# Order of the products in a_out: by pair of heads, or all of one kind first

## The chip, the cores and the metric

The kernel runs on one core of a Trainium2 chip. Five engines work side by side, each on its own list of instructions: TensorE (matrix products; PE in the profile, and PEld for its loads of stationary weights), VectorE (DVE), ScalarE (ACT), GpSimd (POOL) and SyncE (SP, which here issues most of the DMA transfers). They wait for each other by semaphores. SBUF is the working memory, and PSUM, eight banks of 128 x 512 float32, takes the products of TensorE. The metric is device time in microseconds of one execution; less is better.

## The reference

A gated linear recurrence over 768 steps, for 4 batches and 8 heads of size 48, and then two MLPs on its 3072 rows of 384.

```python
for t in range(S):                      # S = 768; state is 48 x 48 for each batch and head
    state = f[:, :, t, :, None] * state + einsum('bhd,bhe->bhde', k[:, :, t], v[:, :, t])
    y[:, :, t] = einsum('bhd,bhde->bhe', q[:, :, t], state)
# x = y as 3072 rows of 384
x = softplus(x @ w_in) @ w_out          # 384 -> 2048 -> 384
x = mish(x @ w_in2) @ w_out2            # the same sizes, mish(h) = h * tanh(softplus(h))
```

f is a sigmoid of f_logit. All is float32.

## The kernel before

**The recurrence in chunks.** A group g is one chunk of 128 steps of one batch; chunk c = g // 4, batch g % 4, 24 groups in all. The eight heads lie as NP = 4 pairs: head 0 of a pair on partitions 0 to 47, head 1 on partitions 64 to 111. Within a group the recurrence is products: `a_scores` (L322) multiplies the scaled k and q of each head, `a_mask` (L335, DVE) keeps the lower triangle of these scores, `a_turn` (L346) and `a_state` (L361) make the contribution to the state, and `a_out` (L384 to L399) makes the outputs y: for each head the product of v with the masked scores (L389: 128 rows of the array, 64 columns, 128 moving columns), and from the second chunk on, added to it in PSUM, the product of the state of the chunk before with q (L397: 48 rows, 48 columns, 128 moving columns). The two heads of a pair write different partitions of one PSUM bank (0 to 63 and 64 to 127), and the four pairs write different columns of that bank. `a_outed` (L424, ACT) copies the bank out when the last product of the group is done. There are 20 groups with c > 0.

**The MLPs in units.** A unit is one layer, one block of 512 tokens and one block of 128 hidden features: 2 x 6 x 16 = 192 units. `m_h` (L467, L481) makes the hidden values, DVE and ACT apply softplus or mish to them and split the result into a high and a low part (`e_hi`, `e_lo`: ghi L496, glo L501), and `m_o` (L601, L611) multiplies these by the output weights. Products of large blocks are made of three products of 12-bit parts; the first eight units and all of the recurrence are plain float32, where every product has two rows on PE and two on PEld. The weights come as float64 bit patterns and are split on DVE and ACT (`split_a`, `split_b`: L139 to L151; `conv_away` for layer 2).

**What sets the order.** The groups of chunk c + 1 are made while the units of token block c run, four groups in the first 12 of 16 units (`plan_attn`: one group in 3 units; its `a_out` stands in the second of these). So the 20 groups with c > 0 lie in units 0 to 79. For these units each engine's list is set by a scheduler from the order in which the code is written and from modelled times; from unit 80 on, and in the steps before the first unit, the order is as written. The four instances of `a_out` for chunk 0 stand in the steps before the first unit and take v alone.

Of the kernel before, what the change touches and what calls it, by code (L numbers as in the profile page):

```python
# [20 lines left out]
NP = H // 2  # L21
# [3 lines left out]
KD = DM // 128  # L25
# [1 line left out]
R = 112  # L27
CAP = 2.0 ** 60
SAFE = 2.0 ** 40
# units are (layer, block of 512 tokens, block of 128 hidden features)  # L30
NAT = 8  # units of the first block whose products are plain float32
SPLITX = 5  # units before NAT at which its input is split
READY = 4  # weight blocks prepared before the first unit
AHEAD = 2  # units between the preparation of a weight block and its use
EARLY = 2  # units between its load and its preparation
LENT = (14, 12, 10, 8) * 3 + (14, 12, 14, 12)  # weight slots that stage a block of layer 1
SPAN = 8  # unit from which layer 2's weights are prepared
LEAD = 2  # units between their load and their preparation
HALVE = 1  # units between the split of a plain float32 block and its use
EVAC = 60  # L40
LAG = 4
LATE = 80  # from this unit on each engine's order is written out
PLACE = (12, 12, 15)
PLACE1 = (3, 3, 12)
HAND = {mybir.EngineType.Activation, mybir.EngineType.DVE, mybir.EngineType.PE}
# what is loaded first, in order: f, q and k ("k"), v of a group, weight block ("w")
LOADS = """
f0 k0 f1 k1 f2 f3 k2 v0 k3 v1 w0 v2 v3 w1 w2 w3 f4 k4 v4 f5 f6
"""
# the steps before the first unit: a letter of one() and a group or weight block  # L50
HEAD = """
h14 e0 P0 s0 e1 q0 P1 i0 s1 e2 k0 S0 q1 i1 P2 e3 k1 S1 p3 s2 i2 m0 o0 O0 h3 b0 q2 k2 S2 s3
i3 R0 m1 o1 O1 q3 k3 S3 m2 y2 A0 B0 O2 b1 R1 m3 y3 O3 b2 R2 C0 A1 B1 b3 R3 C1 t0 t1 A2 B2 T0
# [5 lines left out]
def recurrence__then__softplus_mish_mlps_kernel(  # L59
# [49 lines left out]
    n1 = len(tiles[1])  # L109
    tile_of = {c * B + b0 + j: k for k, (c, b0, nb) in enumerate(tiles[1]) for j in range(nb)}  # L110

    # ---------------------------------------------------------------- weights
    whi, wlo, w32 = {}, {}, {}

    raws = {}
# [17 lines left out]
        raws[layer, f] = raw, win  # L133

    def split_a(layer, f):
        """float64 -> its first 12 significant bits and what float32 keeps of the rest"""
        raw, win = raws[layer, f]
        s, m, sg = raw[:, :, 1], win[:, :, 1], raw[:, :, 0].bitcast(F32)
        act.activation(out=sg, in_=s, func=AF.Sign)  # L139
        dve.tensor_scalar(out=m, in0=m, scalar1=0x1FFFF, scalar2=None, op0=ALU.bitwise_and)  # L140
        dve.tensor_scalar(out=s, in0=s, scalar1=0x7FFFFE00, scalar2=None, op0=ALU.bitwise_and)
        act.activation(out=s, in_=s, func=AF.Relu, scale=8.0, bias=rebias)
# [14 lines left out]
        split_b(layer, f, hi, lo)  # L157

    def whole_a(f):
        """float64 -> float32"""  # L160
        raw, win = raws[1, f]
        s, m, e = raw[:, :, 1], win[:, :, 1], raw[:, :, 0]
        dve.tensor_scalar(out=e, in0=s, scalar1=0x7FF00000, scalar2=None, op0=ALU.bitwise_and)
        dve.tensor_scalar(
            out=m, in0=m, scalar1=0xFFFFFFF, scalar2=0x10000000,
            op0=ALU.bitwise_and, op1=ALU.bitwise_or,
        )
# [38 lines left out]
        whi[layer, f], wlo[layer, f] = w[:, 0], w[:, 1]  # L206
        return w[:, 0], w[:, 1]

    # -------------------------------------------------------------- attention
    G = {}  # L210

    def a_load_f(g):
# [170 lines left out]
    def a_out(g, pl=None):  # L383
        t = G[g]  # L384
        c = g // B
        t["yps"] = ps = bank(pl or ps_a, [128, NP, C])
        for p in range(KD if c == 0 else 0, NP):
            for i in range(2):
                pe.matmul(  # L389
                    ps[64 * i:64 * i + 64, p], t["v"][:, (2 * p + i) * D:(2 * p + i) * D + 64],  # L390
                    t["a", i][:, p],
                    start=True, stop=(c == 0),
                )
            if c:
                for i in (1, 0):
                    o = 64 * i
                    pe.matmul(  # L397
                        ps[o:o + D, p], t["sp"][o:o + D, p], t["q"][o:o + D, p],
                        start=False, stop=True,  # L399
                    )  # L400

    def a_rest(g):
# [39 lines left out]

    states = [const.tile([R, NP, D], F32, name=f"state{b}") for b in range(B)]

    # ------------------------------------------------------------------- MLPs
    xh, xl = {}, {}

    def split_x(key, kk):
# [194 lines left out]

        return [lambda c=c: part(c) for c in range(KD)]

    # --------------------------------------------------------------- schedule
    units = [(layer, k, f) for layer in (1, 2) for k in range(len(tiles[layer])) for f in range(NF)]
    index = {u: i for i, u in enumerate(units)}
    hooks = {}
# [6 lines left out]
            fn()  # L656

    def plan_prep(g, i):
        """the factors of group g over the units i-1 .. i+2"""
        at(i - 1, "act", a_exp, g)  # L660
        at(i, "dve1", a_scan, g)
        at(i, "act", a_inv, g)
        if g + 2 < NC * B:
            at(i, "act", a_load_f, g + 2)
        at(i + 1, "dve1", a_q, g)
        at(i + 2, "dve1", a_k, g)
        at(i + 2, "dve1", a_decay, g)

    def plan_attn(g, i):
        """the products of group g over the units i .. i+2"""  # L670
        at(i, "pe1", a_scores, g)
        at(i, "dve2", a_mask, g, 0)
        at(i, "dve2", a_mask, g, 1)
        at(i + 1, "pe1", a_turn, g)
        at(i + 1, "act", a_turned, g)
        at(i + 1, "pe2", a_out, g)
        at(i + 2, "act0", a_outed, g)
        if g < (NC - 1) * B:
            at(i + 2, "pe1", a_state, g)
            at(i + 2, "dve2", a_stated, g)  # L680
        if g + 2 < NC * B:
            at(i + 2, "dve2", a_load, g + 2)

    for k in range(1, n1):
        c, b0, nb = tiles[1][k]
        base = (k - 1) * NF
        for j in range(nb):
            g, i = c * B + b0 + j, base + 3 * j
# [5 lines left out]
        i = base + 3 * nb  # L694
# [21 lines left out]
    first = [k for k in range(n1) if tiles[1][k][0] > 0][0] * NF  # L716
    last = (n1 - 1) * NF
    for f in range(NF):
        if f >= READY:
            i = f - AHEAD  # L720
            at(max(i - EARLY, -1), "act0", load_w, 1, f)
            at(i, "dve1", whole_w if f < NAT else conv1, f)
        i = first + SPAN + (last - first - SPAN) * f // NF
# [89 lines left out]
    ]  # L813

    def late(i):
        """a unit of the second MLPs, each engine's instructions in the order written"""
        u = units[i] if i < n_units else None
        if u:
            m_h(u)
        t = [U[units[i - j]] if LATE <= i - j < n_units else None for j in range(4)]  # L820
        drain(u, LAG)
        ends = [fn for key in ended for fn in m_end_parts(*key)]
        place = PLACE1 if ended and ended[0][0] == 1 else PLACE
        ended.clear()
        run(i, "act0")
        steps = [
            (t[lag], fn2 if t[lag]["u"][0] == 2 else fn1) if t[lag] else (None, None)
            for lag, fn1, fn2 in STEPS
        ]
        for j, (x, fn) in enumerate(steps):  # L830
            for y, at_step in zip(ends, place):
                if at_step == j:
                    y()
            if x and fn:
                fn(x)
        for y, at_step in zip(ends, place):
            if at_step == len(steps):
                y()
        for where in ("pe1", "dve1", "act", "dve2", "pe2"):
            run(i, where)  # L840
        if u:
            pend.append(u)
# [43 lines left out]
    assert not hooks, sorted(hooks)  # L886
    main.close()

    # ------------------------------------- decays too steep for the products
    redo = nc.values_load(  # L890
        slow[0:1, 0:1], min_val=0, max_val=1, skip_runtime_bounds_check_because="it is 0 or 1"
    )
# [181 lines left out]
```

## Time and profile before

| | |
|---|---|
| median of 3 runs | 963.16 us (962.62 to 964.15) |
| span of the profiled execution, first to last instruction | 960.3 us |
| granted clock of TensorE, mean | 0.999 |
| PE busy, share of the span | 98% |
| DVE busy | 82% |
| ACT busy | 77% |

The profiled execution shows its span alone; the median of the runs lies 2.9 us above it, which is what an execution has around its first and last instruction. A busy PE is not PE at its peak: a product's row lasts until it has left the array, and rows that follow each other overlap, so what a product costs is read from start to start.

### The profile page before, as it was taken

The page shows a single profiled execution, that of the slowest core. Times are in us where ns is not written, and L with a number is a line of the kernel's source. Part 1 is how long each engine was busy: PE and PEld are TensorE (multiplying, and loading weights), DVE is VectorE, ACT ScalarE, POOL GpSimd, SP SyncE. Part 2 cuts the span into 40 slices and gives each one's busy share as a digit, 9 for nine tenths or more (in the row PEclk, how much of TensorE's full clock was granted, in tenths as well). Part 3 has the DMA queues.
Part 4 walks back from the last instruction along what each step waited for, and adds up shares of the span by engine and source line. Part 5 has one row for each costly group of instructions (what it writes and reads, how often), then busy time and mean ns, then how long its engine had stood idle before and what let it go on. Part 6 is the DMA issues. An engine that isn't in the chain of part 4 may idle for free.

```text
span 960.3 us, 13706 instructions
## 1 busy us (share of the span) xinstructions
PE 937.5 (98%) x4970; PEld 721.4 (75%) x4970; DVE 786.1 (82%) x1252; ACT 739.0 (77%) x1326; POOL 29.5 (3%) x84
## 2 busy tenths in 40 slices
PE   4999999999999999999999999999999999999997
PEld 4545767777777777877788888888888888888885
DVE  5999998988888888987677678787787887878875
ACT  4778896888788777866677678887788877887875
POOL 1000000000000000000003220000000000000000
PEclk9999999999999999999999999999999999999999
DMA  9799713354654746463008670100100201000001
GB/s 316 256 327 318 262 46 123 116 191 173 223 178 159 272 148 221 140 230 121 9 38 291 197 241 23 67 34 0 66 34 1 99 1 66 34 1 1 33 0 38
DMA packets 35117, 122.33 MB, mean 127 GB/s; under 512 B 4352, under 2 KB 7424, under 8 KB 35040
## 3 DMA queue, kind: packets, MB, share of 16 engines
q1 hardware_dynamic: 28704, 99.34, 29.8%
q0 software_dynamic: 6336, 22.02, 7.1%
q8 instruction: 41, 0.67, 0.3%
q14 instruction: 36, 0.29, 0.1%
HBM read 93.62 MB, written 26.74 MB: 125 GB/s over the span
## 4 chain that ended last, share of the span: by engine, by line
PE 93%; DVE 4%; issue 1%; ACT 1%; POOL 0%; ACTq 0%; POOLq 0%; DVEq 0%
PE po L611 39%; PE ps L481 39%; PE ps L389 3%; PE ps L397 3%; PE ps L322 2%; PE ps L467 2%; PE po L601 2%; PE ps L361 1%; PE ps L346 1%; PE busy L765 1%; DVE gg L256 0%; DVE a L335 0%; DVE w L147 0%; DVE d L518 0%; PE ps L407 0%
## 5 line engine op out<-in xcount | busy, mean ns | idle before, releaser
L481 PE MATMUL ps<-x,w 128*128 128x512 f32 x864 | 213.6, 392 | 0.0
L611 PE MATMUL po<-ghi,w 128*128 128x512 f32 x768 | 205.4, 398 | 0.0
L481 PEld LDWEIGHTS ps<-x,w 128*128 128x128 f32 x864 | 162.3, 188 | 36.3
L481 PE MATMUL ps<-xh,w 128*128 128x512 f32 x528 | 181.7, 399 | 2.1 <-DVE w L151 1.8
L611 PEld LDWEIGHTS po<-ghi,w 128*128 128x128 f32 x768 | 140.8, 188 | 31.1
L611 PE MATMUL po<-g,w 128*128 128x512 f32 x504 | 126.4, 395 | 0.0
L481 PEld LDWEIGHTS ps<-xh,w 128*128 128x128 f32 x528 | 98.8, 188 | 28.1 <-issue 3.4
L545 ACT ACTIVATE l<-d 128x512 f32<-128x512 f32 x96 | 60.7, 632 | 73.3 <-DVE d L541 73.3
L611 PE MATMUL po<-glo,w 128*128 128x512 f32 x384 | 112.4, 392 | 0.0
L611 PEld LDWEIGHTS po<-g,w 128*128 128x128 f32 x504 | 94.9, 188 | 21.9
L510 ACT ACTIVATE e<-ps 128x512 f32<-128x512 f32 x96 | 57.2, 596 | 70.1 <-PE ps L481 56.2
L481 PE MATMUL ps<-xl,w 128*128 128x512 f32 x264 | 103.1, 391 | 0.0
L501 DVE TENSOR_TENSOR glo<-l,ghi 128x512 fp32r<-128x512 f32 x128 | 87.8, 686 | 17.6 <-ACT ghi L496 16.7
L541 DVE TENSOR_SCALAR d<-ps 128x512 f32<-128x512 f32 x96 | 66.3, 691 | 37.3 <-PE ps L481 37.2
L555 DVE SCALAR_TENSOR_TENSOR l<-d,l 128x512 f32<-128x512 f32 x96 | 66.5, 692 | 33.1 <-ACT l L548 33.0
L496 ACT CAST ghi<-l 128x512 fp32r<-128x512 f32 x128 | 78.1, 610 | 14.4 <-DVE l L531 14.0
L518 DVE SCALAR_TENSOR_TENSOR d<-d,e 128x512 f32<-128x512 f32 x96 | 65.9, 687 | 26.5 <-ACT d L512 26.3
L611 PEld LDWEIGHTS po<-glo,w 128*128 128x128 f32 x384 | 72.1, 188 | 15.9
L578 DVE TENSOR_TENSOR l<-ps,l 128x512 f32<-128x512 f32 x96 | 66.4, 692 | 9.6 <-ACT l L575 0.9
L524 DVE TENSOR_TENSOR d<-l,d 128x512 f32<-128x512 f32 x96 | 65.9, 686 | 2.7
L570 DVE SCALAR_TENSOR_TENSOR l<-d,l 128x512 f32<-128x512 f32 x96 | 65.4, 682 | 0.0
L511 ACT ACTIVATE e<-e 128x512 f32<-128x512 f32 x96 | 60.7, 632 | 1.6
(107 smaller groups left out, 1306.0 us busy)
## 6 DMA issues: line engine op xcount, KB each, us to landing
raw<-in_w_dram SPq DMA_DIRECT2D x32, 768.0 KB, 6.2
w2d<-wo SPq DMA_DIRECT2D x32, 384.0 KB, 3.0
w<-w2d POOLq DMA_DIRECT2D x32, 384.0 KB, 3.9
raw<-in_w_dram SPq DMA_DIRECT2D x16, 767.9 KB, 10.3
win<-in_w_dram SPq DMA_DIRECT2D x16, 767.9 KB, 7.3
qk<-in_qkT_dram SPq DMA_DIRECT2D x22, 448.0 KB, 4.3
x2d<-o SPq DMA_DIRECT2D x12, 768.0 KB, 5.1
x<-x2d POOLq DMA_DIRECT2D x12, 768.0 KB, 5.8
```

What stands on the lines that cost most here:

```text
L481: pe.matmul(ps, w, r, start=(i == 0), stop=(i == len(steps) - 1))
L496: act.copy(out=t["hi"], in_=t["g"])
L501: dve.tensor_tensor(out=t["lo"], in0=t["g"], in1=t["hi"].bitcast(F32), op=ALU.subtract)
L511: act.activation(out=e, in_=e, func=AF.Exp, scale=-1.0)
L518: dve.scalar_tensor_tensor(out=d, in0=d, scalar=1.0, in1=t["e"], op0=ALU.subtract, op1=ALU.subtract)
L524: dve.tensor_tensor(out=d, in0=l, in1=d, op=ALU.subtract)
L541: dve.tensor_scalar(out=t["t"], in0=t["h"], scalar1=20.0, scalar2=None, op0=ALU.min)
L545: act.activation(out=t["l"], in_=t["t"], func=AF.Exp)
L555: dve.scalar_tensor_tensor(out=t["l"], in0=t["t"], scalar=-43.0, in1=t["l"], op0=ALU.max, op1=ALU.add)
L570: dve.scalar_tensor_tensor(out=t["l"], in0=t["t"], scalar=-1.0, in1=t["l"], op0=ALU.mult, op1=ALU.max)
L578: dve.tensor_tensor(out=t["l"], in0=t["h"], in1=t["l"], op=ALU.mult)
L611: pe.matmul(acc[c], w[layer, f][:, cols[c]], t[part], start=(f == 0 and part == "hi" and w is whi), stop=(f == NF - 1 and part == "lo"),)
```

## The change

In a group with c > 0 the eight products of v with the masked scores are issued first, over all four pairs, and then the eight products of the state with q. Before, each pair had its two products of v and then its two of the state. The flags follow: `start` (which makes a product overwrite instead of add) stands on the first pair alone, since it holds for the whole bank, and `stop` on the last. For chunk 0 nothing changes. The diff also takes comments out, which changes no instruction; lines below `a_out` move down by two.

```diff
         t["yps"] = ps = bank(pl or ps_a, [128, NP, C])
-        for p in range(KD if c == 0 else 0, NP):
+        first = 0 if c else KD
+        for p in range(first, NP):
             for i in range(2):
                 pe.matmul(
                     ps[64 * i:64 * i + 64, p], t["v"][:, (2 * p + i) * D:(2 * p + i) * D + 64],
                     t["a", i][:, p],
-                    start=True, stop=(c == 0),
+                    start=(p == first), stop=(c == 0),
                 )
-            if c:
+        if c:
+            for p in range(NP):
                 for i in (1, 0):
                     o = 64 * i
                     pe.matmul(
                         ps[o:o + D, p], t["sp"][o:o + D, p], t["q"][o:o + D, p],
-                        start=False, stop=True,
+                        start=False, stop=(p == NP - 1),
                     )
```

On TensorE, the first group with a state, which stands behind the products of unit 0. Before:

```order
L601 MATMUL po<-g,w_346 128x512
L389 MATMUL ps<-a,vt 64x128 x2
L397 MATMUL ps<-qk,sp 48x128 x2
L389 MATMUL ps<-a,vt 64x128 x2
L397 MATMUL ps<-qk,sp 48x128 x2
L389 MATMUL ps<-a,vt 64x128 x2
L397 MATMUL ps<-qk,sp 48x128 x2
L389 MATMUL ps<-a,vt 64x128 x2
L397 MATMUL ps<-qk,sp 48x128 x2
L361 MATMUL ps<-vt,kn 64x48
```

The same place now:

```order
L603 MATMUL po<-g,w_346 128x512
L390 MATMUL ps<-a,vt 64x128 x8
L399 MATMUL ps<-qk,sp 48x128 x8
L361 MATMUL ps<-vt,kn 64x48
L361 MATMUL ps<-vt,kn 48x48
```

Eight pieces became two; the products are the same, and so are the neighbours on both sides. The same holds for all 20 groups, and nothing else moves on TensorE.

On VectorE the order is the same but for one place, about unit 70, at the last block of layer 2's weights that is split (raw and win are its two copies, wo its parts). Before:

```order
L531 SCALAR_TENSOR_TENSOR l_4293<-ps_4277,d_4294 128x512
L335 TENSOR_TENSOR a_4368<-ps_4343,mask_100 128x512
L501 TENSOR_TENSOR glo_4322<-l_4293,ghi_4320 128x512
L518 SCALAR_TENSOR_TENSOR d_4358<-d_4358,e_4356 128x512
L335 TENSOR_TENSOR a_4370<-ps_4344,mask_100 128x512
L524 TENSOR_TENSOR d_4358<-l_4357,d_4358 128x512
L140 TENSOR_SCALAR win_4554<-win_4554 128x768
L531 SCALAR_TENSOR_TENSOR l_4357<-ps_4333,d_4358 128x512
L141 TENSOR_SCALAR raw_4553<-raw_4553 128x768
```

Now:

```order
L533 SCALAR_TENSOR_TENSOR l_4293<-ps_4277,d_4294 128x512
L141 TENSOR_SCALAR raw_4553<-raw_4553 128x768
L335 TENSOR_TENSOR a_4368<-ps_4343,mask_100 128x512
L503 TENSOR_TENSOR glo_4322<-l_4293,ghi_4320 128x512
L335 TENSOR_TENSOR a_4370<-ps_4344,mask_100 128x512
L140 TENSOR_SCALAR win_4554<-win_4554 128x768
L520 SCALAR_TENSOR_TENSOR d_4358<-d_4358,e_4356 128x512
L147 TENSOR_TENSOR wo_4670<-raw_4553 128x768
```

The steps of that split moved up, the first of them ahead of the first mask of a group; ScalarE's two steps of it (L139, L142) moved up likewise, and on SP's queue one load of v moved ahead of a store of weights.

## Rows read from the trace of the kernel before

**Rows 1.** The page: busy time, and the chain that ended last by engine.

```profile
PE 937.5 (98%) x4970; PEld 721.4 (75%) x4970; DVE 786.1 (82%) x1252; ACT 739.0 (77%) x1326; POOL 29.5 (3%) x84
PE 93%; DVE 4%; issue 1%; ACT 1%; POOL 0%; ACTq 0%; POOLq 0%; DVEq 0%
```

**Rows 2.** Stretches: from:to, length, busy PE, PEld, DVE, ACT, POOL (instructions), clock, DMA.

```profile
48.00:140.00 92.00, 88.97 (x509) 55.07 (x508) 89.20 (x150) 77.36 (x131) 0.45 (x4) 1.00 0.71 249
140.00:230.00 90.00, 90.00 (x563) 67.49 (x562) 81.80 (x135) 71.17 (x131) 0.45 (x4) 1.00 0.42 141
230.00:318.00 88.00, 88.00 (x560) 66.00 (x559) 76.84 (x128) 68.15 (x124) 0.45 (x4) 1.00 0.56 193
318.00:407.00 89.00, 89.00 (x564) 66.84 (x563) 78.45 (x133) 68.58 (x122) 0.83 (x5) 1.00 0.55 191
407.00:475.00 68.00, 68.00 (x412) 50.63 (x411) 50.52 (x80) 44.79 (x82) 0.22 (x2) 1.00 0.36 127
```

**Rows 3.** PE's waits for layer 1's weights, 48 to 475 us: us in total, times, longest.

```profile
PE ps L481 <- DVE w L151: 1.8, 1, 1.8
PE ps L481 <- DVE w L147: 0.3, 1, 0.3
```

**Rows 4.** Timeline of PE, one group's outputs: start us, us, engine, line, operation, shapes, count.

```profile
53.86 0.44 PE L389 MATMUL ps<-a,vt 128*64 128x128 f32 x4
54.23 0.42 PE L397 MATMUL ps<-qk,sp 48*48 48x128 f32 x4
54.58 0.44 PE L389 MATMUL ps<-a,vt 128*64 128x128 f32 x4
...
56.75 0.67 PE L361 MATMUL ps<-vt,kn 128*64 128x48 f32 x16
```

**Rows 5.** PE's instructions by line and shape: count, busy us, mean ns.

```profile
L397 PE MATMUL ps<-qk,sp 48*48 48x128 f32 x320 | 33.8, 288 | 0.0
```

**Rows 6.** Timeline of PE: longer runs of products of one shape, each with the next row.

```profile
31.02 0.86 PE L411 MATMUL ps<-a,qkv 128*48 128x128 f32 x12
31.81 0.98 PE L346 MATMUL ps<-ident,qk 112*128 112x112 f32 x8
...
77.37 1.16 PE L322 MATMUL ps<-qk 48*128 48x128 f32 x16
78.46 2.84 PE L601 MATMUL po<-g,w 128*128 128x512 f32 x6
```

**Rows 7.** Timeline of DVE: its idle time (in brackets) behind late softplus inputs, 48 to 96.

```profile
73.49 0.69 DVE L518 SCALAR_TENSOR_TENSOR d<-d,e 128x512 f32<-128x512 f32 x1 [0.99 <-ACT d L512]
...
80.11 0.69 DVE L518 SCALAR_TENSOR_TENSOR d<-d,e 128x512 f32<-128x512 f32 x1 [0.26 <-ACT d L512]
...
94.00 0.69 DVE L518 SCALAR_TENSOR_TENSOR d<-d,e 128x512 f32<-128x512 f32 x1 [0.21 <-ACT d L512]
```

**Rows 8.** Timeline: a low part as DVE makes it, and PE's first use of it.

```profile
308.90 0.69 DVE L501 TENSOR_TENSOR glo<-l,ghi 128x512 fp32r<-128x512 f32 x1
...
310.72 0.85 PE L611 MATMUL po<-glo,w 128*128 128x512 f32 x3
```

**Rows 9.** Timeline at the moved split: the load of raw, ScalarE's sign, a mask, its use.

```profile
431.11 0.38 SPq L128 DMA_DIRECT2D raw<-in_w_dram  x1
439.36 0.89 ACT L139 ACTIVATE raw<-raw 128x768 f32<-128x768 int32 x1
437.67 0.69 DVE L335 TENSOR_TENSOR a<-ps,mask 128x512 f32<-128x512 f32 x1
444.38 0.44 PE L389 MATMUL ps<-a,vt 128*64 128x128 f32 x4
```

**Rows 10.** DMA issues of 425 to 450 us: count, KB each, median us to landing.

```profile
raw<-in_w_dram SPq DMA_DIRECT2D x1, 768.0 KB, 6.0
```

**Rows 11.** Weight loads of the products of v: count, busy us, mean ns, idle before.

```profile
L389 PEld LDWEIGHTS ps<-a,vt 128*64 128x64 f32 x328 | 16.4, 134 | 19.6 <-issue 14.7 <-DVE raw L141 1.1 <-DVE raw L163 0.8
```

**Rows 12.** A cut of PE's timeline that ends at 55.75 us, inside a state piece.

```profile
55.67 0.31 PE L397 MATMUL ps<-qk,sp 48*48 48x128 f32 x2
```

## The prediction

> **What bounds the kernel now.** I read the page's first lines, then stretches of one token block each, then PE's timeline at one group's outputs, and at last what stands between PE and DVE. The page shows PE busy for 98% of the span and 93% of the chain that ended last on PE [rows 1]. The reader should not stop there, since the change works only from 53.9 to 464 us, and that part has two limits. From 140 to 475 us PE has no idle time at all, while DVE is busy for 81.80 of 90, 76.84 of 88, 78.45 of 89 and 50.52 of 68 us: PE alone sets the pace [rows 2]. From 48 to 140 us it is otherwise: DVE is busy for 89.20 of 92 us, 97%, and PE's only waits of some size, 0.3 and 1.8 us near 128 and 130 us, are for the high and low part of a weight block that DVE splits (L147, L151) [rows 2, 3]. That is a DVE with no room, and a PE that runs a little ahead and is caught at the end of the stretch.
>
> **What the order costs now.** A plain float32 product is two records on PE, and the two heads of a pair run beside each other: a cut in the middle of a state piece shows two records of 0.29 us each within 0.31 us [rows 5, 12]. So a piece of four records is two steps, one behind the other. A v piece takes 54.23 - 53.86 = 0.37 us and a state piece 54.58 - 54.23 = 0.35 us from start to start; the four pairs take 56.75 - 53.86 = 2.89 us [rows 4], that is 4 x 0.72. The same trace has a run of products that stay in one shape: the 12 records of L411 (v and scores again, 48 columns, two heads side by side) are six steps in 31.81 - 31.02 = 0.79 us [rows 6]. Against a state piece, which has the same 48 columns and two steps in 0.35, four steps more cost 0.44 us: 0.11 us for a further step. Two steps at 0.11 would be 0.22; so in every piece some 0.13 to 0.15 us belongs to the change of shape, eight times a group.
>
> **The change, part by part.** The v products become one run of eight steps, 0.37 + 6 x 0.11 = 1.03 us; the state products another, 0.35 + 6 x 0.11 = 1.01 us. Together 2.04 instead of 2.88, or 0.84 us less. There are 320 records of L397 at 16 a group, so 20 groups [rows 5]: 16.8 us less on PE. For the other end I take the longest run of another tiling, the 16 records of the scores, two halves of the rows beside each other: 78.46 - 77.37 = 1.09 us [rows 6]. With both runs at 1.09 the gain is 0.70 a group, 14.0 in all. I take 0.84, since L411 uses the array just as the v products do.
>
> The flags that change sit on the same instructions; I cost them at nothing, and no row lets me price them. The result leaves PSUM behind the last state product, as before, so ACT's copy of y moves with the end of the group.
>
> The moved split on DVE may wait: raw is issued at 431.11 and needs 6.0 us, so it lands near 437.1, and ScalarE's sign of it takes 0.89 us; the first mask behind it started at 437.67 [rows 9, 10]. The wait is about 438.0 + 0.5 for what runs ahead on ScalarE, less 437.6: under 1 us, and the products that read this mask start at 444.38, over 6 us later [rows 9]. Hidden. Without that cover it would be 1 us, once. The load of v that now stands ahead of a weight store on SP holds back a store that only layer 2 reads.
>
> One rule of the Trainium skill speaks against the gain. [rows 6] show that six steps with 128 rows of the array each go on at 0.11 us, weight loads included. The page "TensorE: Matmul & The Clock Gate", Part 3, The mechanism, says that a weight load overlaps matmuls in flight only where their row groups differ, which those of v never do. By that rule each further step would also pay its weight load; the price and time are the slower rival below. The trace does not agree.
>
> **What of it reaches the end.** In the first stretch four groups give PE 3.4 us. PE is then held by DVE, so the end of the stretch comes earlier only by the idle time of DVE that came from a late PE. Three such gaps are plain: ScalarE's 1 + e arrives late, because the hidden values came late, at 73.49, 80.11 and 94.00 us: 0.99 + 0.26 + 0.21 = 1.46 us [rows 7]. Two groups stand ahead of the first two (1.7 us less by then), three ahead of the third, so all three can close. I take 1.5 of 3.4; the ends are 0 and 2.8, all of DVE's idle time there (92 - 89.20 [rows 2]). So 1.9 us turn into a longer wait for L147 and L151 near 128 us.
>
> In the next three blocks PE would need 90, 88 and 89 less 3.4: 86.6, 84.6 and 85.6 us, still above DVE's busy time, by 4.8 us at least [rows 2]. What is late next is the low part glo. It is tightest in the last four units of a block, where no attention slows PE: the closest that I found ends at 308.90 + 0.69 = 309.59, and PE reads it at 310.72, 1.1 us later [rows 8]. DVE has 8.2, 11.2 and 10.6 us idle in these blocks [rows 2], much of it because it waits for products, and can make up most of the 3.4. If half is not made up, 1.7 - 1.1 = 0.6 us of wait comes in that block; I take 0.6 in all. At worst nothing is made up: 3.4 - 1.1 = 2.3 in each of three blocks, 6.9. In the fifth block DVE is at 50.52 of 68, and all passes.
>
> Sum: 16.8 - 1.9 - 0.6 = 14.3 us. The profiled execution's span of 960.3 becomes 946.0; with the 2.9 us that the median of the runs lies above the span, 948.9.
>
> **The rivals.**
> - All of it passes, because DVE's order has more air than its busy share says: 963.2 - 16.8 = 946.4. For it: PE is 98% busy and its waits for weights are 2.1 us in all. Against it: 97% DVE up to 140 us, with the weight split as the last releaser.
> - DVE becomes the bound in the next three blocks too: 16.8 - 1.9 - 6.9 = 8.0 us, 955.2. For it: 91% DVE in the second block, loads and ScalarE that it also waits for. Against it: no wait of PE there now, in over 250 us.
> - Slower: the weights are loaded between the steps, not beside them. Place: the two runs of each group; price: 0.13 us a step (134 ns [rows 11]) on 0.11, so 0.24. A group then takes 0.72 + 12 x 0.24 = 3.60, 0.72 more than now: 963.2 + 14.4 = 977.6. It decides from 0.18 us a step, where 0.72 + 12 x 0.18 = 2.88. Against it: L411 at 0.11.
> - The two heads' state products stop running side by side in the long run, as they share a bank: steps of 0.22, a state run of 0.35 + 6 x 0.22 = 1.67, with 1.03 2.70 a group, gain 0.18 x 20 = 3.6 us: 959.6. Against it: they already run side by side, in that bank [rows 12]. The Trainium skill's page "TensorEngine Tiling (Array Packing)", Gotcha 1: PSUM Pressure, says that different row tiles must not use one bank at the same time, which stands in its way; in this trace they do, on different partitions.
> - The gap between pieces is not the change of shape but what each piece needs anyway, and the run keeps 0.18 us a step: 963.2. Against it: L411 again.
>
> **How the numbers follow.** A run of this kernel tells a change from none at about 0.2%, 1.9 us. Chances: the forecast 0.60 (its own range 946.8, with 2.8 instead of 1.5 in the first stretch and no wait later, to 952), all passes 0.15, DVE bound 0.17, state products one by one 0.03, no gain 0.02, slower 0.03. Faster: 0.60 + 0.15 + 0.17 + 0.03 = 0.95; same 0.02; slower 0.03. The range takes in the first three, from 945.5 to 955.5: below by the error of 0.01 us in each reading (20 groups), above by the case of DVE. The last cases are left out.
>
> **What the profile after would show.** At the outputs of a group: two rows of 16 records, the v run about 1.03 us to the start of the state run, that one 1.01 to the next product. A step at 0.16 or more would speak for the weight loads. Near 128 us PE's wait for L147 and L151 should have grown from 2.1 to about 4 us, and DVE's three gaps should be gone; if PE's wait is as before, the first rival is right. From 140 to 410 us PE should wait for glo or for masks by under 1 us a block, and the blocks should be 3.4 us shorter; waits of 2 us a block mean the second rival. The forecast is wrong from the start if the two runs together take over 2.2 us, or if DVE's order hides a wait that I did not see.

## The result, and the profile after

| | before | changed |
|---|---|---|
| median of 4 runs each | 963.28 us (962.62 to 964.15) | 948.63 us (948.16 to 949.19) |
| ratio | | 0.984, 95% interval 0.983 to 0.986 |
| span of the profiled execution | 960.3 us | 947.2 us |
| that execution's own time | not on record | 948.94 us |

14.65 us went, 1.5%. The forecast was 948.9. In every run here whose time and span are both on record, the time lies 1.65 to 1.82 us above the span. The 2.9 us that "Time and profile before" gives for this compare the span of one execution with the median of others: the profiled execution of the kernel before was some 1.2 us shorter than the median.

The two runs of products came out as the working had them. The timeline of PE at the first group's outputs in the changed kernel (start us, us, engine, line, operation, shapes, count):

```profile
55.47 1.09 PE L390 MATMUL ps<-a,vt 128*64 128x128 f32 x16
56.50 1.08 PE L399 MATMUL ps<-qk,sp 48*48 48x128 f32 x16
57.51 0.67 PE L361 MATMUL ps<-vt,kn 128*64 128x48 f32 x16
```

Read from start to start: 1.03 us for v, 1.01 for the state, 2.04 together, where [rows 4] had 2.89. Over 20 groups that is 17.0 us of PE's time.

The page of the changed kernel, its lines of busy time and of the chain that ended last:

```profile
PE 922.5 (97%) x4970; PEld 727.1 (77%) x4970; DVE 784.7 (83%) x1252; ACT 738.2 (78%) x1326; POOL 29.5 (3%) x84
PE 88%; DVE 7%; issue 2%; ACT 2%; POOL 0%; POOLq 0%; ACTq 0%; DVEq 0%
```

Beside [rows 1], PE is busy for 15.0 us less with as many instructions. DVE has 7% of the chain instead of 4%. The stretches, cut at about the same places of the work as [rows 2]:

```profile
48.00:137.00 89.00, 85.57 (x498) 55.08 (x497) 88.59 (x149) 75.09 (x127) 0.45 (x4) 0.98 0.78 267
137.00:224.00 87.00, 87.00 (x564) 68.78 (x564) 80.73 (x133) 72.18 (x133) 0.45 (x4) 1.00 0.42 140
224.00:309.00 85.00, 85.00 (x561) 67.13 (x560) 76.28 (x127) 68.25 (x125) 0.45 (x4) 1.00 0.56 193
309.00:394.00 85.00, 85.00 (x562) 67.37 (x561) 77.66 (x131) 66.71 (x120) 0.83 (x5) 1.00 0.62 213
394.00:460.00 66.00, 66.00 (x419) 52.69 (x418) 52.37 (x85) 47.24 (x87) 0.40 (x2) 1.00 0.37 131
```

In the first, DVE is busy for 88.59 of 89 us, 99.5%, and PE's granted clock has a mean of 0.98. In the others PE is still never idle, although the blocks are 3.4 to 3.6 us shorter (table below). All that PE waits for between 48 and 475 us in the changed kernel (us in total, times, longest):

```profile
PE ps L483 <- DVE w L151: 2.3, 2, 1.8
PE po L603 <- DVE g L533: 0.9, 1, 0.9
PE ps L483 <- DVE w L147: 0.2, 1, 0.2
```

The second lies at 53 us, ahead of the first group; the kernel before has it too, at 51.5 us. The two others stand for [rows 3]: 2.5 us instead of 2.1. What DVE waits for in this stretch, first in the kernel before and then in the changed one:

```profile
DVE d L518 <- ACT d L512: 1.5, 3, 1.0
DVE glo L501 <- ACT ghi L496: 0.8, 2, 0.5
DVE raw L176 <- ACT raw L171: 0.3, 1, 0.3
```

```profile
DVE glo L503 <- ACT ghi L498: 0.2, 1, 0.2
```

The three gaps of [rows 7], 1.5 us, are gone, and most of the rest too. What is new stands behind the waits. The timeline of PE in the changed kernel, 122 to 137 us (in brackets idle time and what ended it):

```profile
122.72 0.73 PE L483 MATMUL ps<-xh,w 128*128 128x512 f32 x2 [0.55 <-DVE w L151]
...
126.85 0.50 PE L483 MATMUL ps<-xh,w 128*128 128x512 f32 x1 [0.19 <-DVE w L147]
...
129.39 0.73 PE L483 MATMUL ps<-xh,w 128*128 128x512 f32 x2 [1.80 <-DVE w L151]
...
131.30 2.77 PE L613 MATMUL po<-ghi,w 128*128 128x512 f32 x6
...
136.82 1.54 PE L613 MATMUL po<-ghi,w 128*128 128x512 f32 x6
```

The last two rows are the same six products of the same shapes, 2.77 us and 1.54 us. They had nothing to wait for; TensorE ran the first ones at half its clock. In the kernel before the same place of the work had the same wait and the full clock behind it:

```profile
130.52 0.73 PE L481 MATMUL ps<-xh,w 128*128 128x512 f32 x2 [1.80 <-DVE w L151]
...
132.24 1.54 PE L611 MATMUL po<-ghi,w 128*128 128x512 f32 x6
```

The granted clock from 131 to 135 us of the changed execution (columns as in the stretches):

```profile
131.00:135.00 4.00, 4.00 (x13) 3.12 (x12) 4.00 (x7) 3.93 (x9) 0.00 (x0) 0.59 0.00 0
```

The mean of 0.59 over 4 us is mostly 1.2 GHz instead of 2.4.

**Where the gain arises.** The table gives the start of some units in the two profiled executions (first row of the unit's hidden products on PE), and how much earlier the changed kernel is, counted from the start of unit 2. The count starts there because the changed execution came to unit 2 1.6 us later, ahead of the first group with a state. The same kernel run again (e11) came to it at 40.42 us, so this start varies from execution to execution. The spans hold it: they differ by 13.1 us.

| unit | before, us | changed, us | earlier by, us |
|---|---|---|---|
| 2 | 39.72 | 41.33 | 0 |
| 12 | 113.76 | 111.97 | 3.40 |
| 15 | 127.98 | 126.85 | 2.75 |
| 16 | 134.30 | 134.75 | 1.16 |
| 32 | 222.89 | 219.75 | 4.76 |
| 48 | 311.41 | 304.87 | 8.16 |
| 64 | 399.93 | 389.83 | 11.72 |
| 80 | 485.18 | 471.60 | 15.20 |

The first four groups bring all of 4 x 0.85 by unit 12. Of this 0.65 is gone at unit 15: 0.25 at unit 13, where the products with the high part start a little late behind ScalarE, and 0.40 in the waits for split weights of units 14 and 15 (0.55 and 0.19 us now, 0.33 before). From unit 15 to 16, where the wait is 1.80 us in both and the clock is down in one, 1.59 go. Then the four blocks bring 3.60, 3.40, 3.56 and 3.48. The end is 14.7 us earlier.

### The profile page after: what moved, and what is told of

It is laid out like the page before. It is cut to its first block, busy times and chain, and to the rows that moved or that the text cites. A ratio compares the mean times of both kernels' runs of the same rounds, so it can differ in the third digit from the quotient of the medians.

```text
span 947.2 us, 13705 instructions
## 1 busy us (share of the span) xinstructions
PE 922.5 (97%) x4970; PEld 727.1 (77%) x4970; DVE 784.7 (83%) x1252; ACT 738.2 (78%) x1326; POOL 29.5 (3%) x84
## 4 chain that ended last, share of the span: by engine, by line
PE 88%; DVE 7%; issue 2%; ACT 2%; POOL 0%; POOLq 0%; ACTq 0%; DVEq 0%
PE po L613 40%; PE ps L483 39%; PE ps L322 2%; PE ps L390 2%; PE ps L399 2%; PE ps L361 1%; PE ps L346 1%; PE ps L469 1%; DVE d L526 1%; PE busy L767 1%; DVE gg L256 1%; DVE a L335 1%; DVE w L147 1%; DVE d L520 1%; DVE raw L176 0%
## 5 line engine op out<-in xcount | busy, mean ns | idle before, releaser
L503 DVE TENSOR_TENSOR glo<-l,ghi 128x512 fp32r<-128x512 f32 x128 | 87.7, 685 | 14.2 <-ACT ghi L498 13.6
L514 ACT ACTIVATE d<-e 128x512 f32<-128x512 f32 x96 | 60.7, 632 | 1.7
```

Of the source, the lines that this page charges most:

```text
L503: dve.tensor_tensor(out=t["lo"], in0=t["g"], in1=t["hi"].bitcast(F32), op=ALU.subtract)
L514: act.activation(out=d, in_=e, func=AF.Identity, bias=1.0)
```

## The experiments

All gains below are read in the same way from the profiled execution of each kernel: us earlier than before at the start of a unit, counted from unit 2. Medians are of timed runs, and each stands beside the kernel before in runs of the same chip (963.28 us for the first row, 963.7 to 964.1 for the others); across chips, compare the ratios. In e4 to e8 the scheduler also put some of PE's products of units 13 to 20 in another order, so the columns 15 to 20 of these rows tell of that order too.

| kernel | 12 | 15 | 16 | 20 | 32 | 48 | 64 | 80 | end | median, us |
|---|---|---|---|---|---|---|---|---|---|---|
| changed | 3.40 | 2.75 | 1.16 | 2.11 | 4.76 | 8.16 | 11.72 | 15.20 | 14.69 | 948.63 |
| e1, two by two | 2.31 | 1.94 | 0.46 | 1.15 | 2.92 | 5.28 | 7.61 | 9.93 | 9.40 | 953.31 |
| e2, staggered | 1.15 | 1.08 | 1.09 | 1.36 | 2.27 | 3.47 | 4.67 | 5.81 | 5.84 | 959.11 |
| e3, filler | 3.38 | 2.56 | 2.25 | 3.20 | 5.85 | 7.98 | 9.72 | 13.20 | 12.71 | 949.63 |
| e4, changed, less DVE | 3.39 | 3.44 | 6.33 | 5.66 | 7.71 | 10.44 | 10.73 | 14.21 | 13.73 | 950.86 |
| e5, before, less DVE | 0 | 0.65 | 3.54 | 1.98 | 2.00 | 2.00 | 2.00 | 2.00 | 1.73 | 961.49 |
| e6, before, more DVE | 0 | -1.36 | -2.99 | 0.45 | -2.91 | -3.86 | -3.85 | -3.85 | -4.31 | 968.79 |
| e7, early split | 3.35 | 2.48 | 5.97 | 6.94 | 4.91 | 6.13 | 7.46 | 10.93 | 10.26 | 952.21 |
| e8, loads on POOL | 2.70 | 1.75 | 1.30 | 0.77 | -8.38 | -15.99 | -22.53 | -19.05 | -19.30 | 986.17 |
| e9, lead of 3 | 3.38 | 2.72 | 2.72 | 3.59 | 5.52 | 5.16 | 5.38 | 8.85 | 8.49 | 956.97 |
| e9, lead of 4 | 3.39 | 2.74 | 1.14 | 2.10 | 3.94 | 5.19 | 7.46 | 10.96 | 10.40 | 953.55 |
| e10, lead of 3 and filler | 3.38 | 2.57 | 2.69 | 3.61 | 4.70 | 5.85 | 2.29 | 5.77 | 5.41 | 956.02 |
| e11, changed again | 3.41 | 2.72 | 1.15 | 2.11 | 4.76 | 8.29 | 11.46 | 14.96 | 14.82 | 949.46 |

### What a piece costs: two by two, and staggered

The changed kernel's products, in two other orders. `with_v(p)` and `with_state(p, last)` issue the two products of one pair. In both, VectorE, ScalarE and SP keep the order of the kernel before: the split at unit 70 does not move.

```diff
+            steps = "v0 v1 s0 s1 v2 v3 s2 s3".split()      # e1_two_by_two
+            steps = "v0 v1 s0 v2 s1 v3 s2 s3".split()      # e2_staggered
+            for z, step in enumerate(steps):
+                if step[0] == "v":
+                    with_v(int(step[1]))
+                else:
+                    with_state(int(step[1]), z == len(steps) - 1)
```

> Order v0 v1, s0 s1, v2 v3, s2 s3 (v and s are a pair's two products with v and with the state): four pieces a group instead of eight before and two in the changed kernel. Theory, a fixed price of 0.143 us for each change of shape: a group takes 4 x 0.143 = 0.57 us less than before, 20 groups 11.4, so 951.9, or 953.5 if TensorE's clock falls near 131 us as in the changed kernel; a piece of four steps takes 0.37 + 0.22 = 0.59 (v) and 0.57 (state). Rival, the gap is a state product's wait for the v product just before it in the same columns: no such neighbours are left, so the full gain of the changed kernel, 948.6.

> Order v0 v1, s0, v2, s1, v3, s2 s3: six pieces a group, and no state product stands right behind the v product of its own columns. Theory, a price for each change of shape: two changes fewer than before, 2 x 0.143 x 20 = 5.7 us, so 957.6. Rival, the wait for the same columns: as the changed kernel, 948.6.

Two by two took 953.31 us (952.73 to 955.51), ratio 0.990 (0.988 to 0.992); staggered 959.11 us (956.85 to 960.22), ratio 0.995 (0.994 to 0.997). PE's timeline at the first group, two by two:

```profile
54.59 0.66 PE L391 MATMUL ps<-a,vt 128*64 128x128 f32 x8
55.18 0.64 PE L400 MATMUL ps<-qk,sp 48*48 48x128 f32 x8
55.75 0.66 PE L391 MATMUL ps<-a,vt 128*64 128x128 f32 x8
...
56.91 0.67 PE L361 MATMUL ps<-vt,kn 128*64 128x48 f32 x16
```

And staggered:

```profile
54.44 0.66 PE L391 MATMUL ps<-a,vt 128*64 128x128 f32 x8
55.03 0.42 PE L400 MATMUL ps<-qk,sp 48*48 48x128 f32 x4
55.38 0.44 PE L391 MATMUL ps<-a,vt 128*64 128x128 f32 x4
...
57.04 0.67 PE L361 MATMUL ps<-vt,kn 128*64 128x48 f32 x16
```

A group takes 56.91 - 54.59 = 2.32 us in four pieces and 57.04 - 54.44 = 2.60 in six. With 2.89 in eight and 2.04 in two, each piece that goes is worth 0.14 us, whichever columns stand behind each other. In neither order does a state product stand right behind the v product of its own columns, and the group still pays for each piece. So the price is not the sum in PSUM on columns just written. Nor is it the change of operands and bank alone: the MLPs' products of 12-bit parts change both without changing shape, and go on at 0.23 us from start to start. In the changed kernel:

```profile
113.80 0.39 PE L483 MATMUL ps<-xh,w 128*128 128x512 f32 x1
114.03 1.54 PE L613 MATMUL po<-ghi,w 128*128 128x512 f32 x6
115.41 0.85 PE L613 MATMUL po<-glo,w 128*128 128x512 f32 x3
```

(1.38 us for six, 0.23 for the one ahead of them.) That leaves the change between the two shapes of `a_out`; other pairs of shapes were not tried. At unit 80 staggered has 5.81 us, 20 x 0.29.

The times: two by two came to the 953.5 that was named for a clock that falls, and from unit 15 to 16 it loses 1.48 us. Staggered came out 1.5 us above its 957.6. Its two runs with a mean clock of 0.998 took 956.85 and 957.37 us, its three with 0.996 took 959.1 to 960.2. Both are far from the rival's 948.6.

### The clock: zero products in the gaps

Two products of 128 columns ahead of unit 14's hidden products and eight ahead of unit 15's, with a block of zeros (`none`), added to the bank without changing it. They run while PE would be idle. The scheduler moved four of the sixteen records of one group's scores (L322) into the same places; otherwise every engine keeps the order of the changed kernel.

```diff
+FILL = {(1, 0, 14): 2, (1, 0, 15): 8}
...
+            if i == 1:
+                for z in range(FILL.get(u, 0)):
+                    pe.matmul(ps[:, 0:128], ident, none, start=False, stop=False)
```

> The changed kernel with products of a zero block, which add nothing, in two hidden-value products of the first block: two at unit 14 and eight at unit 15 (0.22 us each, 0.43 and 1.7 us), in the place where TensorE waits for the low part of a weight block (0.55 and 1.80 us). Nothing becomes ready earlier. Theory, these idle stretches made the clock fall to half from 130.9 to 134.3 us: the clock stays at 1.00 and the time falls by 1.6 us to 947.0. Rival, the clock has nothing to do with it or falls for another reason (the longer runs of small products): the clock still falls and the time stays at 948.6, or rises by what the filler exceeds the waits.

The median is 949.63 us (949.05 to 950.69), ratio 0.985 (0.984 to 0.987). The first stretch of that kernel (columns as before):

```profile
48.00:137.00 89.00, 87.78 (x523) 57.73 (x522) 88.61 (x149) 76.24 (x129) 0.45 (x4) 1.00 0.74 264
```

The clock stays at 1.00, and the kernel is 1.09 us ahead of the changed one at units 16 and 32. From unit 15 to 16 it loses 0.31 us where the changed one loses 1.59; 0.19 more it had lost by unit 15. So in these executions the filler costs 0.5 us and saves 1.6. The clock came out as the theory had it, and the time, 949.63 instead of 947.0, did not. The lead goes: 7.98 against 8.16 at unit 48, 9.72 against 11.72 at unit 64. PE's waits in this kernel and the rows that lead to one of them:

```profile
PE po L618 <- ACT ghi L503: 2.4, 3, 1.5
```

```profile
376.23 0.89 ACT L141 ACTIVATE raw<-raw 128x768 f32<-128x768 int32 x1 [2.25 <-DMA raw<-in_w_dram]
377.15 0.56 DVE L143 TENSOR_SCALAR raw<-raw 128x768 int32<-128x768 int32 x1 [2.17 <-ACT raw L141]
...
385.30 1.65 PE L618 MATMUL po<-ghi,w 128*128 128x512 f32 x6 [1.52 <-ACT ghi L503]
```

A load of layer 2's weights lands, ScalarE has stood for it for 2.25 us and DVE for 2.17, and the high part of the hidden values behind them on ScalarE comes late. In the changed kernel the same load ended shorter waits:

```profile
374.05 0.89 ACT L139 ACTIVATE raw<-raw 128x768 f32<-128x768 int32 x1 [0.86 <-DMA raw<-in_w_dram]
374.96 0.56 DVE L141 TENSOR_SCALAR raw<-raw 128x768 int32<-128x768 int32 x1 [0.77 <-ACT raw L139]
```

ScalarE waits for these loads for 6.1 us between 225 and 400 us in the changed kernel and 8.9 with the filler. The clock's cost could be bought back, and bought nothing at the end. That it was the filler that kept the clock up rests on more than this one execution, since the clock also held once without it (below): the four runs with the filler have mean clocks of 0.997 to 0.999, the changed kernel's eight 0.995 to 0.998. It is no guarantee: with the filler and a lead of 3 two of five runs are at 0.995 and 0.996.

### DVE's share: less of it in both orders, more of it in the old one

Eight weight blocks of layer 1 are split with one step of DVE less: the mask of L140 is left out for them, and the bits that it clears stay in. This once with the changed order (e4) and once with the old one (e5). And the other way, the old order with that mask three times for blocks 14 and 15 (e6).

```diff
-        dve.tensor_scalar(out=m, in0=m, scalar1=0x1FFFF, scalar2=None, op0=ALU.bitwise_and)
+        if layer == 2 or not deep:                                          # e4, e5
+        for z in range(3 if layer == 1 and deep and f in (14, 15) else 1):  # e6
+            dve.tensor_scalar(out=m, in0=m, scalar1=0x1FFFF, scalar2=None, op0=ALU.bitwise_and)
```

> The changed kernel without one step of VectorE (the mask of the low bits, L140) in the split of layer 1's eight weight blocks: about 8 x 0.5 = 4 us less on VectorE before 130 us; the low parts of these weights are then not what they should be. Theory, the first stretch is held by VectorE: the waits for L151 (2.3 us) shrink, the clock stays up, and unit 16 starts 2 us or more earlier against unit 2 than in the changed kernel. At the end 944 to 947, if the later blocks keep it. Rival, the 2.2 us of the first stretch were lost to the clock alone: 1.1 to 1.6 us come back and no more.

> The same step left out of the kernel before. Theory, VectorE's room decides what the first four groups are worth: between this kernel and the changed one with the same step left out, the whole 3.4 us of four groups appear by unit 16 (1.2 between the two full kernels). Time 960.5 to 963. Rival, the loss in the first stretch is not VectorE's: about 1.2 here too.

> The kernel before, its outputs by pair, with the step L140 three times instead of once in the split of the last two weight blocks (the result is the same): 4 x 0.47 = 1.9 us more on VectorE. Theory, the clock falls because TensorE idles: its waits for L147 and L151 grow from 2.1 to about 3 to 4 us and the clock falls near 131 us here too, 2 to 3 us slower. Rival, the clock falls because of the long runs of small products: it stays at 1.00 as in the kernel before.

With less DVE the changed order takes 950.86 us (948.93 to 952.30), ratio 0.987 (0.986 to 0.989), and the old one 961.49 us (959.80 to 962.69), ratio 0.998 (0.997 to 0.999). The edit is not the only difference: the scheduler put many steps of DVE, ACT and SP in another order, from 78 us on and into the later blocks. e4 and e5 share that order but for `a_out` and two issues on SP, so they are compared with each other. One step less on DVE gives the old order 2.00 us by unit 32, about what PE had waited for weights in [rows 3], and nothing after. PE's waits for these weights shrink to 0.5 us in the changed order and 0.3 in the old one, and the clock stays. The difference of the two orders at unit 15 is 3.44 - 0.65 = 2.79 us, as in the kernels with the whole mask (2.75); but at unit 16 it is still 6.33 - 3.54 = 2.79, not 1.16, and at unit 32 7.71 - 2.00 = 5.71, not 4.76. So the fallen clock was what the new order had lost on top. The theory had the whole 3.4 us by unit 16; 0.6 of it did not come, and the time missed its 944 to 947. But with less DVE the changed order's block 4 (units 48 to 63) brings only 0.29 us, and the end is no better than that of the changed kernel. PE's waits in this kernel (e4), and the same chain:

```profile
PE po L614 <- ACT ghi L499: 3.7, 5, 1.8
```

```profile
373.17 0.90 ACT L139 ACTIVATE raw<-raw 128x768 f32<-128x768 int32 x1 [2.46 <-DMA raw<-in_w_dram]
374.10 0.56 DVE L142 TENSOR_SCALAR raw<-raw 128x768 int32<-128x768 int32 x1 [3.18 <-ACT raw L139]
378.43 1.66 PE L614 MATMUL po<-ghi,w 128*128 128x512 f32 x6 [1.83 <-ACT ghi L499]
```

With more DVE the old order took 968.79 us (one run, so no ratio). The clock falls there too, without the new runs of sixteen products. The waits are not those expected: for split weights they shrink to 1.4 us, and 2.5 us are for high parts, in an order that the scheduler changed from 117 us on. Its PE, with the idle time ahead of the fall, and the clock:

```profile
131.73 0.50 PE L482 MATMUL ps<-xh,w 128*128 128x512 f32 x1 [1.11 <-DVE w L148]
...
134.31 0.50 PE L612 MATMUL po<-ghi,w 128*128 128x512 f32 x1 [1.84 <-ACT ghi L497]
```

```profile
135.00:139.00 4.00, 4.00 (x13) 3.10 (x12) 4.00 (x7) 3.53 (x6) 0.00 (x0) 0.57 0.00 0
```

So the new order is not what lowers the clock; idle time of PE stands ahead of it in both orders. The kernel lost 3.85 us by unit 48, more than the 2.99 at unit 16.

### The split of two weight blocks earlier

The changed kernel with the splits of blocks 14 and 15 put forward in the scheduler's order.

```diff
-        split_w(1, f, *w_tiles(1, f))
+        if f in (14, 15):
+            with tc.high_priority(offset=60):
+                split_w(1, f, *w_tiles(1, f))
+        else:
+            split_w(1, f, *w_tiles(1, f))
```

> The changed kernel, with VectorE's and ScalarE's split of the last two weight blocks of layer 1 (units 14 and 15) ahead in priority, three rows of VectorE's list earlier. Theory, the waits for these blocks cost 2.5 us and the fallen clock 1.6: both waits shrink by one to two us and the clock stays up, 945.5 to 947.0. Rival, VectorE has no room in this stretch, and what it does earlier here is late elsewhere (low parts, masks): new waits of the same size, 948.6.

The median is 952.21 us (950.97 to 952.32), ratio 0.988 (0.986 to 0.989). The waits for these blocks shrink to 0.2 us and the clock stays. At unit 32 the kernel is 4.91 us ahead, 0.15 more than the changed one; at unit 48 it stands 2.0 behind it. Its time lies outside both the theory and the rival. PE's waits:

```profile
PE po L613 <- ACT ghi L498: 4.8, 6, 2.0
```

The largest of these waits, 2.03 and 1.23 us, stand at 299.5 and 381.9 us, in blocks where DVE is busy for 89% (76.27 of 86 and 77.37 of 87 us). So the rows do not show the rival's cause, a DVE without room, at that place. The order of DVE, ACT and SP differs from the changed kernel's into these blocks; which step made the high parts late is not shown.

### The loads of layer 2's weights: another queue, or earlier

If an early PE gains nothing because the loads of layer 2's weights come late, then loads at another place should help: on GpSimd's queue, or three or four units ahead of their split instead of two; and three with the filler. The changed kernel was run again beside them.

```diff
-        nc.sync.dma_start(out=raw.rearrange("p m z -> p (m z)"), in_=src.bitcast(I32))
+        q = nc.gpsimd if layer == 2 and deep else nc.sync             # e8_pool_loads
+        q.dma_start(out=raw.rearrange("p m z -> p (m z)"), in_=src.bitcast(I32))
...
-LEAD = 2
+LEAD = 3                                                              # e9_lead3, e10
+LEAD = 4                                                              # e9_lead4
+FILL = {(1, 0, 14): 2, (1, 0, 15): 6}                                 # e10, as in e3
```

> The changed kernel with the loads of layer 2's weights issued by GpSimd instead of SyncE, where they stand behind loads of q that wait for a group's outputs. Theory, what the later blocks lack is the time of these loads (ScalarE waits for them and the high parts stand behind): ScalarE's wait for raw, 6.1 us from 225 to 400 us, falls under 2, and the time by 0 to 1 us, since TensorE did not wait there. Rival, GpSimd's transfers come later or in each other's way, and the order that the scheduler then picks costs more: 949 to 953.

> The changed kernel with layer 2's weight blocks loaded three units before their split instead of two (LEAD = 3): more of these loads stand ahead of the loads of q that wait for a group's outputs. Theory, the next thing late after the products is this load (ScalarE and VectorE wait for it by up to 2.8 us, and in two versions of the changed kernel TensorE then waited for the high parts): ScalarE's wait for raw from 225 to 400 us falls from 6.1 to under 3 us and TensorE never waits for ghi, 947 to 948.6. Rival, the other order that the scheduler picks puts splits where VectorE has no room: waits for ghi of 2 to 5 us, 950 to 953.

> The same with LEAD = 4. Theory as for LEAD = 3, with the loads further ahead: 946.5 to 948.6. Rival: 950 to 953.

> LEAD = 3 with two and six zero products in the waits of units 14 and 15. Theory, the clock stays up, which is worth 1.1 us at unit 32 in the version with fillers alone, and earlier loads keep it in the later blocks: 946 to 947.5. Rival, it is given back in waits for ghi in the third and fourth block: 948.6 or more.

> The changed kernel again, on the chip of the three versions above, as their measure: ratio to the kernel before 0.984, clock fallen near 131 us.

| | median, us | range | ratio, interval |
|---|---|---|---|
| loads on POOL | 986.17 | 983.61 to 987.04 | 1.024, 1.022 to 1.026 |
| lead of 3 | 956.97 | 954.46 to 958.91 | 0.993, 0.991 to 0.994 |
| lead of 4 | 953.55 | 951.63 to 953.86 | 0.988, 0.987 to 0.990 |
| lead of 3 and filler | 956.02 | 954.48 to 956.80 | 0.991, 0.990 to 0.993 |
| changed again | 949.46 | 947.97 to 951.09 | 0.985, 0.984 to 0.987 |

None helps. The first three took longer than even their rivals had said (953), the fourth is as its rival said, and the repeat came out as expected. On GpSimd's queue the loads came late: ScalarE waits for them for 41.3 us in all. They took no longer from issue to landing (median 5.9 us, 6.1 on SP's queue in the changed kernel), so they were issued late. What held them there I did not follow. PE's waits in that kernel:

```profile
PE po L614 <- ACT ghi L499: 13.3, 6, 4.9
...
PE ps L347 <- DVE a L336: 10.2, 7, 3.0
```

A lead of 3 or 4 changes the order of DVE, ACT and SP from about 185 us on; PE's order stays. With 4, ScalarE waits for the loads for only 2.6 us in 225 to 400 us, instead of 6.1, and PE still waits 1.5 us for ghi and 1.2 for masks; with 3 (ScalarE 8.7) it is 2.6 and 2.4. So the loads are not the only thing that comes late there. That part of the theory failed.

In e10 PE waits 5.1 us for ghi and 2.7 for masks, as its rival said. The leads of 3 and 4 showed something else. Up to 184 us the two have the order of the changed kernel on every engine. The timeline of PE with a lead of 3:

```profile
129.58 0.74 PE L483 MATMUL ps<-xh,w 128*128 128x512 f32 x2 [1.81 <-DVE w L151]
...
131.29 1.54 PE L613 MATMUL po<-ghi,w 128*128 128x512 f32 x6
```

And with a lead of 4:

```profile
130.00 0.73 PE L483 MATMUL ps<-xh,w 128*128 128x512 f32 x2 [1.81 <-DVE w L151]
...
131.88 2.77 PE L613 MATMUL po<-ghi,w 128*128 128x512 f32 x6
```

The same wait of 1.81 us stands ahead of both; in one execution the clock held (1.00 from 132 to 136 us), in the other it fell (0.51 from 131.5 to 135). At unit 15 both are 2.7 us ahead, at unit 16 2.72 and 1.14: the fall costs 1.58 us there.

## Why the prediction was right, and where it was not

**PE's saving: right.** Forecast 1.03 and 1.01 us for the two runs, measured 1.03 and 1.01; 16.8 us against 17.0. The price of a change of shape, 0.13 to 0.15 us, is 0.14 by four orders. The slower rival is refuted: the eight steps of v, 128 rows each, go on at (1.03 - 0.37) / 6 = 0.11 us, although their sixteen weight loads of 0.13 us [rows 11] add up to 2.1. The rule of the Trainium skill's page "TensorE: Matmul & The Clock Gate", Part 3, The mechanism, that a weight load overlaps only where the row groups differ, does not hold in this trace. The Trainium skill's page "TensorEngine Tiling (Array Packing)", Key Properties, says that a change of the tiling mode drains TensorE, and gives no price. The trace agrees that a change of shape costs, 0.14 us each time; what TensorE does in that time it does not show. The rival of the shared bank is refuted by the state run of 1.01 us.

**The first stretch: total near, the step wrong.** The step read "1.9 us turn into a longer wait for L147 and L151 near 128 us", with 1.5 of 3.4 us passing. DVE gave more: 2.75 us had passed at unit 15, near the upper end of 2.8, all of DVE's idle time. I had counted only the three plain gaps, 1.5 us: that term was too small. DVE waited for 2.6 us in all before and 0.2 after, and ended at 99.5% busy. PE's waits for L147 and L151 grew from 2.1 to 2.5, not to 4. Then TensorE's clock fell to 1.2 GHz behind these waits and took 1.59 us. The prediction had no clock in it, since before it was 1.00 in every stretch that I read, in one execution. By unit 16 the loss is 3.40 - 1.16 = 2.24 us against the 1.9 forecast: a size that was right by luck, for another reason. The test that I named, "near 4 us of wait", would have spoken for the first rival (all passes), wrongly.

**The next three blocks: the 0.6 us did not come.** PE does not wait for glo or masks between 137 and 460 us. But the margin is smaller. The closest that I found in the changed kernel, which answers [rows 8]:

```profile
303.04 0.69 DVE L503 TENSOR_TENSOR glo<-l,ghi 128x512 fp32r<-128x512 f32 x1
...
304.18 0.85 PE L613 MATMUL po<-glo,w 128*128 128x512 f32 x3
```

It is ready 0.45 us before its use, instead of 1.1. So DVE made up nearly all, where I had let half be lost. The place was right, as other kernels show: the large waits of e3 (385.3 us), e4 (378.4) and e7 (299.5 and 381.9) lie in the last four units of a block. But what came late there was the high part from ScalarE, not glo. Every kernel that came to unit 32 earlier than this one (e3, e4, e7, lead of 3) had such waits; so had some that came later (lead of 4, e10), so that being early is their cause is shown at most for e3, where hardly anything else moved. The second rival, DVE as the bound in these blocks, did not happen here: PE waits for DVE's masks (1.2 to 10.2 us) only in the four kernels whose loads were moved.

**The moved split: hidden, as costed.** Its first step on DVE waits for 0.26 us, under the 1 us named, and the products that read the mask behind it start at 432.53 us, over 5 us later:

```profile
426.80 0.56 DVE L141 TENSOR_SCALAR raw<-raw 128x768 int32<-128x768 int32 x1 [0.26 <-ACT raw L139]
```

From unit 64 to 80 the gain is 3.48 us, all that four groups save.

**Sum.** Measured from unit 2: 17.0 - 0.65 (late weights and high part) - 1.59 (clock) + 0.4 (more in blocks 2 to 5 than 16 x 0.85 = 13.6) - 0.5 (after unit 80) = 14.7, against 16.8 - 1.9 - 0.6 = 14.3. Two terms that were too pessimistic, by 1.25 and 0.6, and the unexplained 0.4 stood for two that were missing, the clock and the end. That the sum came within 0.4 us is in part luck; the saving on PE is not. The 2.9 us around the span stand on both sides of the forecast and change nothing in it.

**Slips in the working.** PE has a third wait of some size in the first stretch before, 0.9 us at 51.5 us; it lies ahead of the first group and costs the argument nothing. The lower end of the forecast's own range, 946.8, comes out of its terms as 947.0, and the 0.01 us a reading that is named for the range's lower end gives 946.2, not 945.5.

**What stays open.** Why blocks 2 to 5 bring 0.4 us more than the groups save, and what takes 0.5 behind unit 80. Why the clock falls in one execution and not in another with the same waits. What exactly makes ghi late with longer leads. And in how many of the timed runs the clock fell: a mean clock does not tell by itself, since the traces also end at half clock, with PE idle (the last 2.0 us of the kernel before, 4.0 of the changed one). But the 32 runs of the kernel before beside the experiments differ by it: 21 with 0.996 or 0.997 take 964.2 us in the mean, 11 with 0.998 or 0.999 take 963.3. Its profiled execution, with 0.999, is like the second kind. So the clock probably falls in many runs of the old order too, where PE has the same wait of 1.80 us; no trace shows it. If it does, less of the 1.59 us stands between the two medians than between these two executions.

## What to carry to other kernels

Small products of different array shapes are worth sorting by shape: each change between 128x64 and 48x48 cost 0.14 us here, and a step in an unbroken run 0.11. Price the saving on the engine first, then take for each stretch no more than the idle time of the engine that feeds it: with DVE at 97%, 2.75 of 3.4 us passed, and none of the attempts to win the rest ended sooner: in each, PE then waited for high parts in later blocks. Where a saving shortens TensorE's cover and lets it stand idle, read the granted clock behind that wait as well as the wait.

## What the runs showed of the hardware that was not expected

- TensorE's granted clock fell to 1.2 GHz after idle times of 0.55, 0.19 and 1.80 us between 122 and 129.4 us, in which PE was otherwise at work, and six products of 128 x 512 then took 2.77 us instead of 1.54. In the old order with more DVE it fell after 0.30, 1.11 and 1.84 us.
- The same idle time did not always bring it: 0.55, 0.20 and 1.81 us ahead of the same products, once with the clock at 0.51 behind them, once at 1.00. After 0.33 and 1.80 us (the kernel before) and after 0.23, 0.16 and 1.80 (staggered) it stayed at 1.00.
- With zero products in the gaps it stayed at 1.00 in the profiled execution, at a price of 0.5 us.
